# Moving routing steps inside the attention phase of a two-block kernel, with its inputs loaded four items ahead

## The chip, the cores and the metric

The kernel runs on one NeuronCore of a Trainium2 chip. The metric is the device time of one execution in microseconds (us). The engines are named as in the profile: PE is TensorE (the matrix engine; PEld is its weight loading), DVE is VectorE, ACT is ScalarE, POOL is GpSimd, SP is SyncE, which here only issues transfers. SBUF is the on-chip memory of 128 partitions, PSUM the accumulator memory that PE writes.

## The reference

Two blocks follow one another. The first is a linear attention with a decaying state (4 batches, 8 heads, 768 tokens, head size 48). The second is a mixture of 8 experts in which a token either takes the expert with the largest logit, or keeps the expert of the token before it.

```python
for t in range(S):                                  # attention, per batch and head
    cur = einsum('bhd,bhe->bhde', u * k[t], v[t])
    y[t] = einsum('bhd,bhde->bhe', r[t], state + cur)
    state = w * state + einsum('bhd,bhe->bhde', k[t], v[t])
x = y as (B, S, H*D)                                # 4 x 768 tokens of 384
...
logits = x @ w_gate                                 # 8 per token
local_gate = sigmoid(x @ w_local)
for b, s:                                           # the choice of an expert
    fresh_e = argmax(logits[b, s])
    e = fresh_e if s == 0 or local_gate[b, s] < 0.5 else prev_e
    prev_e = e
    p = softmax(logits[b, s])
    out[b, s] = p[e] * (relu(x[b, s] @ w1[e]) @ w2[e])
```

## The kernel before

The order of all work is written out by hand: each engine executes its instructions in the order in which the program emits them, and waits by semaphores for the others.

**Attention** (class Attention, method run) works through 16 items; an item is one batch and two heads. The loop runs over steps n = 0 to 16. Step n finishes item n-1 (`inside`, line L297; `before`, L310, whose result ACT copies at L318), turns the output of item n-2 (`turn`, L329, copied by ACT at L331), makes the score products of item n+1 (`scores`, L288, masked by DVE into the tile `am`, L290), starts item n's output (`own`, L267, multiplied by DVE into `y`, L273), scales keys two items ahead (`keys`, DVE, tile `kw`, L236), makes per-chunk sums (`added`, PE, L248, into a part T of the PSUM tile `mp`) and scans them to states (`states`, DVE, tile `S`, L254). POOL does `scale` for the next item: `rw` (L229), `ke` (L212) and `pd` (L216), two instructions each. The scores and the turned outputs share two PSUM banks (`pair`), so `turn` (L329) can only start once DVE has masked the scores that lay in its bank.

**Loads.** SP issues three transfers per item: `rk`, `kv`, `vT` (L194, L198, L199). `AHEAD` is the depth: there are AHEAD buffers of `rk` and of `vT` and AHEAD+1 of `kv`, and step n issues the loads of item n+AHEAD-1. In the kernel before AHEAD is 3. The queue is in order: a load whose buffer isn't free holds up those behind it.

**Routing** (class Router). Logits of a batch are made by PE every fourth step (`logits`, L342, then `token_logits`, L348 and the DVE reduction L349). Batches 0 and 1 form group 0, and its routing is spread over the steps 9 to 15 (g = 8 in the code): step 9 `experts_of` part 0 (L688 maximum, into `mp`; L689 comparison; L691 ACT copy of the maximum; L692 product with the table `down`), and part 1 (L694 to L696); step 10 `keys` (transposition L703) and `runs` (a scan, L708, from PSUM); step 11 `turn_runs` (L713, into `mp`), `last` (L720) and `one_hot` (L727 to L731); step 12 `counts` (two products, L740 and L741) and `ranks` (L747 to L756); step 13 `slots` (L792 to L795) and `columns` (tile `eqv`, L800); then `places` (tile `ohq`, L811, in two halves), `numbers` (tile `val`, L805, on POOL in step 14) and in step 15 `summed` (L818), `head` (L828 to L849) and the gather of the first expert's rows (L1077). Tables of whole numbers (`ie`, `iq`, `ij`, `down`, `t8`, `t1`, `tie`, `ief`) are made by POOL with iota instructions (L623) in steps 3, 4 and 5 (method `constants`), and cast to float by ACT in step 6 (L678).

**Experts** (class Experts) begin with the first gathered rows (transposed at L1090), products L1104, L1191, L1154, L1223, rows written by POOL (L1303). Group 1 (batches 2 and 3) is routed by the same methods while the first experts run. Weights of the first expert are loaded by SP in steps 14 and 15 (L1066).

Of the kernel before, what the change touches and what calls it, by code (L numbers as in the profile page):

```python
# [14 lines left out]
Alu = mybir.AluOpType  # L15
# [5 lines left out]
P = 128  # L21
# [5 lines left out]
E, F = 8, 1024  # L27
DK, FK = D // P, F // P
NCH = S // P
NC = B * NCH  # L30
N = B * S

ST = 4
# [4 lines left out]
EARLY = 2  # L38
HEAD = 192
TAIL = 256  # L40
# [8 lines left out]

W_LO, W_HI = 0.8, 1.25  # L50
C2 = NCH // 2
AHEAD = 3
VB = NCH * 2 * DH


def spread(ap, axis, n):

    a = ap.unsqueeze(axis)
    return a.to_broadcast([n if i == axis else s for i, s in enumerate(a.shape)])


class Attention:
# [289 lines left out]
    def run(self, router, fetch, heads):  # L352


        def pair(name):
            t = self.banks(name)
            return [t[:, 0], t[:, 1]]

        M = B * HP

        mp, mp_end = router.mp, 2 * P + 2 + (NCH - 1) * DH

        g = GROUPS[0][1] * HP
        for n in range(M + 1):
            if n + AHEAD - 1 < M:
                self.load(n + AHEAD - 1)
            if n == 0:
                self.scale(0)
                self.keys(0)
                self.tables()  # L370
                self.scores(0, 0)()
                self.scores(0, 1)()
                self.own(0)
                self.nc.scalar.copy(self.first, self.tab[:, 1, 0])
                self.turn_ends(slice(1, HP))
                self.warm(3)
                self.added(0)
                self.reciprocals(1)
                self.states(0)
                self.scale(1)  # L380
                continue
            if n < 3:

                self.keys(n)
                self.inside(n - 1)
                self.before(n - 1)
                if n == 2:
                    self.turn(0, pair("tp"))
                self.nc.scalar.copy(self.first, self.tab[:, n + 1, 0])
                self.scores(n, 0)()  # L390
                keep = self.scores(n, 1)
                self.own(n)
                keep()
                self.added(n)
                self.states(n)
                if n == 1:
                    self.reciprocals(2)
                self.scale(n + 1)
                continue
            if n < M:  # L400
                self.turn(n - 2, pair("tp"))
                if n >= M - 2:
                    fetch(2 * (n - M + 2))
                if n == 3:
                    self.reciprocals(3)
                if n < 5:
                    self.keys(n)
                if n > 3:
                    if n not in (g + 3, g + 5):
                        self.added(n)  # L410
                    self.states(n)
            if n == 4:
                self.keys(5)
            if n > HP and n % HP == 1:
                self.token_logits(n // HP - 1, pair("lq")[0])
            if n == g + 1:
                router.experts_of(0, (0,))
            if n == g + 5:
                router.slots(0)
                router.columns(0)  # L420
            if n == M:
                router.shares(0)
            if n + 1 < M:
                self.scale(n + 1)
            if n == g + 6:
                router.numbers(0, self.nc.gpsimd)
            if 3 <= n < 6:
                router.constants(n - 3)
            if n == M:
                self.turn(M - 2, [self.spare[:, 0], self.spare[:, 1]])  # L430
            self.inside(n - 1)
            if n == g + 3:

                router.turn_runs(0, mp[:, mp_end:])
            self.before(n - 1)
            if M - 2 <= n < M:
                fetch(2 * (n - M + 2) + 1)
            if n == 6:
                router.cast()
            if n == M:  # L440
                break
            if n == g + 3:
                router.last(0, mp[:, mp_end:])
                router.one_hot(0, (0,))
            if n == g + 7:

                router.summed(0, 0)
                router.copied(0, self.nc.vector.tensor_copy)
                self.spare = self.py.tile([P, 2, 512], F32, name="y")
                router.head(self.spare[:, 0])  # L450
                heads()

            ahead = n if n < 5 else n + 1
            if n == 3:
                self.added(3)
                self.states(3)
            if ahead < M:
                self.scores(ahead, 0)()
                keep = self.scores(ahead, 1)
            if n % HP == 0:  # L460

                keep()
                self.own(n)
                self.logits(n // HP - 1, pair("lp")[0])
                if n == 4:
                    self.scores(5, 0)()
                    self.scores(5, 1)()
                    self.keys(6)
                if n == g + 4:
                    self.added(n + 1)  # L470
                    router.counts(0, [mp, mp[:, E * NC // 2:]])
                    router.ranks(0, (0,))
                if n > 4:
                    self.keys(n + 2)
                if n == g + 4:
                    router.ranks(0, (1,))
            else:
                self.own(n)
                if n == g + 2:
                    self.added(n + 1)  # L480
                    router.keys(0, mp)
                    router.runs(0)
                if 4 < n < M - 2:
                    self.keys(n + 2)
                if ahead < M:
                    keep()
            if n == g + 1:
                router.experts_of(0, (1,))
            if n == g + 3:
                router.one_hot(0, (1,))  # L490
            if n == g + 5:
                router.places(0, 0)
            if n == g + 6:
                router.places(0, 1)
        self.inner.close()
# [81 lines left out]
class Router:  # L577
# [43 lines left out]
    def iota(self, name, shape, pattern, base=0, cm=0, cast=False):  # L621
# [5 lines left out]
        self.casts.append((f, i))  # L627
        return f

    def constants(self, part):  # L630
        nc = self.nc
        if part == 0:
            self.ie = self.iota("ie", [P, E], [[1, E]])
            self.iq = self.iota("iq", [P, P], [[1, P]])
            self.ij = self.iota("ij", [P, E * ST], [[1, E * ST]])
            self.ones = self.tl("r_ones", [P, P])
            nc.vector.memset(self.ones, 1.0)
        elif part == 1:
            self.down = self.iota("down", [P, E], [[-1, E]], base=E, cast=True)

            self.t8 = self.iota("t8", [P, NC], [[E * P, NC]], base=2 * E, cm=E, cast=True)
            self.t1 = self.iota("t1", [P, NC], [[P, NC]], base=1, cm=1, cast=True)
        else:

            c = self.g[0]["nc"]
# [5 lines left out]
            nc.vector.memset(self.go, 1.0)  # L651
            nc.vector.memset(self.go.rearrange("p (b c) -> p b c", c=NCH)[:, :, NCH - 1:], 0.0)
            nc.vector.memset(self.g[0]["ext"][:, :, 0:1], 0.0)

            self.tie = self.tl("tie", [P, E])
            for x, (z, base) in enumerate(((slice(0, EARLY), E - 1 - E * TAIL), (slice(EARLY, E), E - 1 - EARLY))):
                i = self.iota(f"tie{x}", [P, z.stop - z.start], [[-1, z.stop - z.start]], base=base)
                self.casts.append((self.tie[:, z], i))
            self.ief = self.iota("ief", [1, E], [[1, E]], cast=True)

            self.size = self.tl("size", [1, E])
            for i, n in enumerate(BLOCKS):
# [18 lines left out]
    def experts_of(self, i, parts=(0, 1)):  # L681

        nc, g, lt = self.nc, self.g[i], self.lt
        lg = lt[:, g["z"], :E]
        if 0 in parts:
            nc.vector.memset(lt[:, g["z"]].rearrange("p (b c) e -> p b c e", c=NCH)[0:1, :, 0, E:], -1.0)
            mx = self.mp[:, :g["nc"]] if i == 0 else g["mx"]
            nc.vector.tensor_reduce(mx, lg, axis=AX.X, op=Alu.max)  # L688
            nc.vector.tensor_tensor(g["eq"], lg, spread(mx, 2, E), op=Alu.is_equal)  # L689
            if i == 0:  # L690
                nc.scalar.copy(g["mx"], mx)  # L691
            nc.vector.tensor_tensor(g["eq"], g["eq"], spread(self.down, 1, g["nc"]), op=Alu.mult)  # L692
        if 1 in parts:
            nc.vector.tensor_reduce(g["k"], g["eq"], axis=AX.X, op=Alu.max)  # L694
            nc.vector.tensor_tensor(g["k"], self.t8[:, g["z"]], g["k"], op=Alu.subtract)
            nc.vector.scalar_tensor_tensor(g["key"], lt[:, g["z"], E], FRESH_TO, g["k"],  # L696
                                           Alu.is_le, Alu.mult)
# [1048 lines left out]
```

## Time and profile before

| what | value |
|---|---|
| median of 3 runs | 384.6 us (382.99 to 389.75) |
| the profiled execution's own time | 384.6 us |
| its span, first to last instruction | 382.8 us |
| mean granted TensorE clock | 0.995 |
| busy: PE | 366.8 us (96%) |
| busy: DVE | 251.9 us (66%) |
| busy: POOL | 151.9 us (40%) |
| busy: ACT | 107.3 us (28%) |
| moved by DMA | 74.97 MB, mean 196 GB/s |

The profiled execution has the time of the median; 1.8 us of it lie outside the span. The busy time of PE is modelled from pipelined products, so a busy PE is not always PE at its best. Attention takes the first 112 us or so; the experts' first products (L1104) start at 115.03 us.

### The profile page before, as it was taken

The page shows a single profiled execution, that of the slowest core. Times are in us where ns is not written, and L with a number is a line of the kernel's source. Part 1 is how long each engine was busy: PE and PEld are TensorE (multiplying, and loading weights), DVE is VectorE, ACT ScalarE, POOL GpSimd, SP SyncE. Part 2 cuts the span into 40 slices and gives each one's busy share as a digit, 9 for nine tenths or more (in the row PEclk, how much of TensorE's full clock was granted, in tenths as well). Part 3 has the DMA queues.
Part 4 walks back from the last instruction along what each step waited for, and adds up shares of the span by engine and source line. Part 5 has one row for each costly group of instructions (what it writes and reads, how often), then busy time and mean ns, then how long its engine had stood idle before and what let it go on. Part 6 is the DMA issues. An engine that isn't in the chain of part 4 may idle for free. (4 is left out here: it accounts for less than half of the span.)

```text
span 382.8 us, 9693 instructions
## 1 busy us (share of the span) xinstructions
PE 366.8 (96%) x3846; PEld 324.0 (85%) x3846; DVE 251.9 (66%) x720; ACT 107.3 (28%) x295; POOL 151.9 (40%) x213
## 2 busy tenths in 40 slices
PE   8999999889999999999999999999999999999992
PEld 7776777666769988999999999999999899899971
DVE  6888778988944646496566857758758758466400
ACT  4132232223222211322323333233234233232210
POOL 7769999887222042411432313213313113012022
PEclk9999999999999999999999999999999999999998
DMA  7999899977566880830561254145246146064011
GB/s 254 412 410 377 300 340 323 374 283 276 191 208 218 324 341 16 309 120 22 207 207 62 57 188 197 54 172 206 76 165 228 37 176 229 10 216 169 3 37 36
DMA packets 17765, 74.97 MB, mean 196 GB/s; under 512 B 2761, under 2 KB 6618, under 8 KB 15408
## 3 DMA queue, kind: packets, MB, share of 16 engines
q1 hardware_dynamic: 10336, 56.89, 40.4%
q0 software_dynamic: 3424, 9.52, 7.5%
q10 hardware_dynamic: 3952, 7.87, 5.7%
q8 instruction: 32, 0.52, 0.5%
q14 instruction: 21, 0.17, 0.2%
HBM read 64.83 MB, written 9.51 MB: 194 GB/s over the span
## 5 line engine op out<-in xcount | busy, mean ns | idle before, releaser
L1303 POOL DMA_INDIRECT out_dram<-yo,sid x27 | 26.7, 987 | 102.3 <-ACT yo L1298 78.9
L1154 PE MATMUL h<-exT,w1t 128*128 128x168 f32 (+4 forms) x240 | 54.9, 327 | 0.0
L1158 DVE TENSOR_TENSOR hT<-h,hs 128x168 f32<-128x168 f32 (+3 forms) x60 | 21.1, 351 | 46.5 <-PE h L1154 31.0
L1077 POOL DMA_INDIRECT xg<-x_d,gid x29 | 31.1, 1074 | 37.1 <-DVE sm L900 17.4
L1154 PEld LDWEIGHTS h<-exT,w1t 128*128 128x128 f32 x240 | 41.6, 190 | 0.3 <-issue 0.3
L1104 PE MATMUL h<-exT,w1t 128*128 128x192 f32 (+1 forms) x192 | 38.3, 338 | 0.0
L1223 PE MATMUL y<-factors,sums 128*128 128x192 f32 x168 | 36.8, 326 | 0.0
L1154 PE MATMUL h<-xs,ws 128*128 128x168 f32 (+4 forms) x144 | 35.2, 326 | 0.0
L216 POOL TENSOR_TENSOR pd<-rk 128x384 f32<-128x384 f32 x32 | 31.5, 1004 | 6.8 <-PE y L267 5.6
L290 DVE TENSOR_TENSOR am<-pair,kept 128x768 f32<-128x768 f32 x32 | 30.0, 951 | 5.9 <-PE pair L288 5.6
L1104 PEld LDWEIGHTS h<-exT,w1t 128*128 128x128 f32 x192 | 32.2, 190 | 1.5 <-issue 0.2
L1154 PEld LDWEIGHTS h<-xs,ws 128*128 128x128 f32 x144 | 25.5, 190 | 4.3 <-ACT hs L1161 1.2
L1223 PEld LDWEIGHTS y<-factors,sums 128*128 128x128 f32 x168 | 28.9, 190 | 0.0
L212 POOL TENSOR_TENSOR ke<-kv,endT 128x288 f32<-128x288 f32 x32 | 25.1, 803 | 1.5 <-DMA kv<-in_kv_dram 1.1
L229 POOL TENSOR_TENSOR rw<-rk,tab 128x384 f32<-128x384 f32 x26 | 23.8, 936 | 4.1 <-DMA rk<-in_rk_dram 4.1
L297 PE MATMUL y<-am,kv 128*64 128x128 f32 x360 | 23.9, 277 | 0.8 <-DVE y L273 0.8
L288 PE MATMUL pair<-rw,kw 48*64 48x128 f32 (+1 forms) x768 | 23.3, 250 | 1.1 <-DVE lt L349 0.6
L1223 PE MATMUL y<-w2t,hT 128*128 128x192 f32 x96 | 23.0, 328 | 0.0
L1091 DVE COPY exT<-tp 128x384 f32<-128x384 f32 (+6 forms) x29 | 14.0, 489 | 13.6 <-PE tp L1090 13.4
L288 PEld LDWEIGHTS pair<-rw,kw 48*64 48x64 f32 x768 | 19.5, 133 | 3.5 <-issue 1.9
L297 PEld LDWEIGHTS y<-am,kv 128*64 128x64 f32 x360 | 19.9, 137 | 2.4 <-DVE y L273 1.0
L318 ACT COPY xT<-y 128x768 f32<-128x768 f32 x15 | 12.0, 800 | 33.7 <-PE y L310 33.7
(300 smaller groups left out, 741.7 us busy)
## 6 DMA issues: line engine op xcount, KB each, us to landing
w1t<-in_w_dram SPq DMA_DIRECT2D x8, 1536.0 KB, 6.7
w2t<-in_w_dram SPq DMA_DIRECT2D x8, 1536.0 KB, 7.5
rk<-in_rk_dram SPq DMA_DIRECT2D x15, 768.0 KB, 7.4
kv<-in_kv_dram SPq DMA_DIRECT2D x16, 584.0 KB, 7.1
vT<-in_vT_dram SPq DMA_DIRECT2D x16, 384.0 KB, 6.7
x_d<-x ACTq DMA_DIRECT2D x4, 1152.0 KB, 4.6
w1t<-in_w_dram SPq DMA_DIRECT2D x2, 768.0 KB, 4.6
w2t<-in_w_dram SPq DMA_DIRECT2D x2, 768.0 KB, 4.5
```

The lines of the kernel that those rows point to most:

```text
L212: nc.gpsimd.tensor_mul(t["ke"][:, p::2], t["k"][:, p::2], spread(self.endT[:, p, hp], 1, C2))
L216: nc.gpsimd.tensor_mul(t["pd"][:, z], t["rT"][:, z], t["kT"][:, z])
L229: engine.tensor_mul(t["rw"][:, z], t["rT"][:, z], spread(pw, 1, z.stop - z.start))
L288: nc.tensor.matmul(sc[f * DP:(f + 1) * DP, h, i, x:], lhsT=t["kw"][q, c, o * DP:(o + 1) * DP], rhs=t["rw"][q, c, x:], start=True, stop=True)
L290: return lambda: nc.vector.tensor_mul(t["am"][:, g], sc, spread(self.kept[:, g:g + 3], 1, 2))
L297: nc.tensor.matmul(t["y"][h][p * DP:(p + 1) * DP, c2 * P:(c2 + 1) * P], lhsT=t["v"][:, (2 * c + h) * DH:(2 * c + h) * DH + DP], rhs=t["am" ...
L1077: self.nc.gpsimd.indirect_dma_start(out=xg[:n], out_offset=None, in_=self.x_d[:rows], in_offset=bass.IndirectOffsetOnAxis(ap=u["gid"][:n, ...
L1104: nc.tensor.matmul(h[:, :n], lhsT=u["w1"][:, m, kk, :], rhs=u["xT"][:, kk, :], start=(kk == 0), stop=(kk == DK - 1))
L1154: nc.tensor.matmul(out, lhsT=a, rhs=b, start=start and k == 0, stop=stop and k == len(terms) - 1, skip_group_check=True)
L1158: nc.vector.tensor_tensor(out, a, b, op=Alu.add)
L1223: return lambda: nc.tensor.matmul(bank[:, x * half:(x + 1) * half], lhsT=a, rhs=b, start=(j == 0 and x == 0), stop=(j == FK // 2 - 1), ski ...
L1303: self.nc.gpsimd.indirect_dma_start(out=out.rearrange("n (h d) -> (n h) d", h=2) if half else out, out_offset=bass.IndirectOffsetOnAxis(ap ...
```

## The change

Six things are altered:

- AHEAD becomes 4: one more buffer of `rk`, `vT` and `kv`, and each load is issued one step earlier in the program; the load of `wp` (weights of the logits) comes after the loads of item 2.
- In `experts_of` for group 0 the result of the comparison (L689) goes to PSUM, into a free part of `mp`, and the product (L692) reads it there.
- The scan of states of item 11 (step 11) is emitted in step 10, right behind the scan `runs`.
- In step 12 `added` and `counts` are emitted ahead of `logits`.
- In step 13 `columns` (`eqv`) moves from the start of the step to its end, behind the second masking, and the first half of `places` moves from there into step 14, behind the scan of states.
- All iota tables are made in step 2, between `states` and `scale`, in a method `numbering`; `constants` keeps its DVE memsets in steps 3 and 5.

```diff
-AHEAD = 3
+AHEAD = 4
...
                 if n == 1:
                     self.reciprocals(2)
+                else:
+                    router.numbering()
                 self.scale(n + 1)
...
                     if n not in (g + 3, g + 5):
                         self.added(n)
-                    self.states(n)
+                    if n != g + 3:
+                        self.states(n)
...
             if n == g + 5:
                 router.slots(0)
-                router.columns(0)
...
             if n == g + 6:
                 router.numbers(0, self.nc.gpsimd)
-            if 3 <= n < 6:
+                router.places(0, 0)
+            if n in (3, 5):
                 router.constants(n - 3)
...
                 self.own(n)
+                if n == g + 4:
+                    self.added(n + 1)
+                    router.counts(0, [mp, mp[:, E * NC // 2:]])
                 self.logits(n // HP - 1, pair("lp")[0])
...
                 if n == g + 4:
-                    self.added(n + 1)
-                    router.counts(0, [mp, mp[:, E * NC // 2:]])
                     router.ranks(0, (0,))
...
                     router.keys(0, mp)
                     router.runs(0)
+                    self.states(n + 1)
...
             if n == g + 5:
-                router.places(0, 0)
+                router.columns(0)
...
+    def numbering(self):
+        self.ie = self.iota("ie", [P, E], [[1, E]])
+        self.iq = self.iota("iq", [P, P], [[1, P]])
+        self.ij = self.iota("ij", [P, E * ST], [[1, E * ST]])
+        self.down = self.iota("down", [P, E], [[-1, E]], base=E, cast=True)
+        self.t8 = self.iota("t8", [P, NC], [[E * P, NC]], base=2 * E, cm=E, cast=True)
+        self.t1 = self.iota("t1", [P, NC], [[P, NC]], base=1, cm=1, cast=True)
+        self.tie = self.tl("tie", [P, E])
...
+        self.ief = self.iota("ief", [1, E], [[1, E]], cast=True)
...
-            nc.vector.tensor_tensor(g["eq"], lg, spread(mx, 2, E), op=Alu.is_equal)
+            eq = self.mp[:, g["nc"]:g["nc"] * (E + 1)].rearrange("p (c e) -> p c e", e=E) if i == 0 else g["eq"]
+            nc.vector.tensor_tensor(eq, lg, spread(mx, 2, E), op=Alu.is_equal)
             if i == 0:
                 nc.scalar.copy(g["mx"], mx)
-            nc.vector.tensor_tensor(g["eq"], g["eq"], spread(self.down, 1, g["nc"]), op=Alu.mult)
+            nc.vector.tensor_tensor(g["eq"], eq, spread(self.down, 1, g["nc"]), op=Alu.mult)
```

More of the change, by code (lines that the diff above doesn't have):

```diff
@@ L628, in iota @@
         return f
+    def numbering(self):
[6 more added lines that the diff above has]
+        self.tie = self.tl("tie", [P, E])
+        for x, (z, base) in enumerate(((slice(0, EARLY), E - 1 - E * TAIL), (slice(EARLY, E), E - 1 - EARLY))):
+            i = self.iota(f"tie{x}", [P, z.stop - z.start], [[-1, z.stop - z.start]], base=base)
+            self.casts.append((self.tie[:, z], i))
+        self.ief = self.iota("ief", [1, E], [[1, E]], cast=True)
     def constants(self, part):
@@ L632, in constants @@
         if part == 0:
-            self.ie = self.iota("ie", [P, E], [[1, E]])
-            self.iq = self.iota("iq", [P, P], [[1, P]])
-            self.ij = self.iota("ij", [P, E * ST], [[1, E * ST]])
             self.ones = self.tl("r_ones", [P, P])
             nc.vector.memset(self.ones, 1.0)
[L638 to L642, printed above, removed]
         else:
@@ L653, in constants @@
             nc.vector.memset(self.g[0]["ext"][:, :, 0:1], 0.0)
[L655 to L659, printed above, removed]
             self.size = self.tl("size", [1, E])
```

## The prediction

> **What bounds the kernel now.** I first cut the span into stages by the busy time of each engine. Columns: stretch, its length, then busy time and instruction count of PE, PEld, DVE, ACT, POOL, then granted clock, DMA share, GB/s.
>
> ```profile
> 0.00:115.00 115.00, 106.91 (x2203) 81.76 (x2203) 91.63 (x167) 32.19 (x81) 87.93 (x124) 1.00 0.86 312
> 115.00:376.00 261.00, 259.91 (x1645) 242.22 (x1643) 160.29 (x554) 75.10 (x214) 63.02 (x88) 1.00 0.42 149
> 376.00:382.80 6.80, 0.00 (x0) 0.00 (x0) 0.00 (x0) 0.00 (x0) 0.97 (x1) 0.73 0.09 21
> ```
>
> The experts (115 to 376 us) leave PE idle for 1.1 us of 261: PE sets their length, and an earlier start of them is an earlier end. The change touches nothing there. In attention PE is idle for 8.1 us of 115, and only there can a new order win. So I cut attention into steps, from the first `before` product (L310) of a step to that of the next one: steps 9 to 14.
>
> ```profile
> 66.40:72.71 6.31, 5.31 (x128) 4.19 (x126) 6.31 (x6) 1.50 (x3) 5.37 (x7) 1.00 1.00 356
> 72.71:79.27 6.56, 5.66 (x131) 4.47 (x129) 6.17 (x11) 1.50 (x3) 4.98 (x7) 1.00 0.99 371
> 79.27:85.80 6.53, 5.67 (x129) 4.51 (x129) 5.13 (x8) 1.88 (x5) 6.28 (x8) 1.00 0.66 250
> 85.80:93.40 7.60, 7.60 (x151) 5.46 (x150) 5.85 (x8) 2.22 (x5) 6.89 (x9) 1.00 0.70 257
> 93.40:100.17 6.77, 5.41 (x129) 4.32 (x127) 6.53 (x16) 1.57 (x4) 3.21 (x4) 1.00 0.53 183
> 100.17:105.45 5.28, 5.28 (x129) 4.24 (x127) 4.77 (x6) 1.65 (x5) 0.00 (x0) 1.00 0.84 282
> ```
>
> Step 14 (last row) has PE busy throughout and takes 5.28 us, as do the plain steps 6 and 7 (L310 at 48.56, 53.84, 59.12): that is PE's own floor. Step 12 carries the logits and counts and also has no idle PE. Steps 9 and 13 have DVE nearly full and PE waiting: there DVE is the bound. In the timeline I then looked for what PE waits for, and what DVE does ahead of it.
>
> ```profile
> 65.85 1.68 POOL L229 TENSOR_TENSOR rw<-rk,tab 128x384 f32<-128x384 f32 x2
> 66.13 3.03 DVE L692 TENSOR_TENSOR eq<-eq,down 128x96 f32<-128x96 f32 x1
> 67.50 1.54 POOL L212 TENSOR_TENSOR ke<-kv,endT 128x288 f32<-128x288 f32 x2
> 70.08 0.79 PE L329 MATMUL pair<-ident,xT 112*128 112x112 f32 x6 [1.00 <-DVE am L290]
> ...
> 79.11 0.23 PE L713 MATMUL mp<-ident,run 12*128 12x12 f32 x1 [0.90 <-DVE inc L726]
> 83.17 0.79 PE L329 MATMUL pair<-ident,xT 112*128 112x112 f32 x6 [0.86 <-DVE am L290]
> 91.41 1.08 DVE L748 TENSOR_TENSOR_SCAN exc<-seg,ext 128x104 f32<-128x104 f32 x1 [1.52 <-ACT ext L747]
> 95.38 0.77 PE L288 MATMUL pair<-rw,kw 48*64 48x128 f32 x24 [0.63 <-DVE lt L349]
> 96.05 0.56 DVE L800 TENSOR_TENSOR eqv<-si,ij_i 128x384 f32<-128x384 int32 x1
> 97.53 0.80 PE L329 MATMUL pair<-ident,xT 112*128 112x112 f32 x6 [0.73 <-DVE am L290]
> ...
> 115.67 0.26 DVE L689 TENSOR_TENSOR eq<-lt,mx 128x96 f32<-128x96 f32 x1
> 115.96 0.26 DVE L692 TENSOR_TENSOR eq<-eq,down 128x96 f32<-128x96 f32 x1
> ```
>
> The reader is to see that L692 takes 3.03 us at 66.13 and 0.26 us at 115.96, where POOL does nothing. The long one ends (69.16) just after POOL's unbroken row of `rw` and `ke` (69.04). Its two inputs both lie in SBUF. DVE instructions with one input in PSUM stay at their time beside a busy POOL: the scans L254 between 60 and 112 us take 0.630 to 0.655 us. PE's waits for DVE in these steps add up to 1.00 + 0.90 + 0.86 + 0.63 + 0.73 = 4.12 us. That is the stock that this change can draw on.
>
> **The change part by part.**
>
> *Comparison in PSUM (step 9).* Instruction counts stay; L692 now has one SBUF input. At 0.26 instead of 3.03 us, DVE is 2.77 us earlier. As built, L692 now also waits for ACT's copy L691 (0.17 us), so some 0.2 comes off. PE had waited 1.00, and the step exceeds the floor by 6.31 - 5.28 = 1.03: gain 1.00. Bounds: 0, if L692 is slow for another reason, and 1.03. The rest of the 2.77 makes DVE punctual in step 10, behind it.
> [...]
>
> *Scan behind the runs (steps 10, 11).* The transposition L713 writes `mp` and waited 0.90 us until DVE had done the scan L254 (78.42 to 79.05), though PE was free at 78.2 and `runs` was done at 76.78. With the scan right behind `runs` it ends at 76.78 + 0.64 = 77.42, before PE is free: gain 0.90. Queued behind it on DVE are `kw` and one masking, 0.64 us later each, done by about 79.1; the next to need them is L288 at 80.42, less the 0.90. Hidden, with 0.4 us of cover. The wait of 0.86 in step 11 stands behind L728 and L729, which take 0.68 and 0.72 us there against 0.17 alone; they collide with `ke` on POOL, and that is changed by nothing here except its timing. Between 0 and 0.86, I take 0.3, nearer the row as it is.
>
> *Counts in front of logits (step 12).* The order on PE changes, not its work. The logits hold it for 1.50 us (L342 from 88.41), so the counts come that much earlier and the 1.52 us in which DVE waits for `ext` go. But behind it come L754 to L756 (0.25, 0.18 and 0.26 us), with SBUF inputs, and `ke` holds POOL from 92.22 to 93.85: they may end where they end now. Logits come 0.8 us later; ACT's copy (0.48 us) then ends about when L348 is due, 91.5, so this costs up to 0.1.
>
> *`eqv` behind the masks (steps 13, 14).* It frees 0.56 us ahead of the masking for which PE waits 0.73, and puts them into step 14, where DVE has 5.28 - 4.77 = 0.51 us free. There `ohq` (0.95 us) may also stand behind `val` on POOL, which now can't begin before `eqv` and takes 0.83. Together with the counts: at best all of 0.63 + 0.73 = 1.36 goes and step 14 gives back 0.05, so 1.3; at worst only 0.56 goes and 0.05 + 0.83 comes back, so -0.3. Of these I take 0.6, near the middle. What becomes late next is the masking at the start of step 14, and L329 behind it.
>
> *Tables in step 2.* Nine iotas take 0.40 + 0.29 + 0.26 = 0.95 us of POOL by their rows at 33.44, 38.94 and 44.62. They move into this wait:
>
> ```profile
> 22.25 1.69 POOL L229 TENSOR_TENSOR rw<-rk,tab 128x384 f32<-128x384 f32 x2 [2.25 <-DMA rk<-in_rk_dram]
> ```
>
> They cost nothing there. If the load came earlier and took that cover away, POOL's `pd` of item 3 would end 0.95 later than 27.38, still before its use at 29.07. In steps 3 to 5 POOL gains 0.95, but no matrix product waits for POOL: taken as 0, at most 0.6 (weight loads waited that long for `ke`).
>
> *Four items ahead.* No bytes are added: an item is 768 + 584 + 384 = 1736 KB. POOL waits for loads 4.1 (`rw`), 1.2 (`pd`) and 1.1 us (`ke`) in all, and those go. But POOL is ahead: the `rw` that waits 1.15 us at 79.02 is used by PE at 86.33. Gain 0. On SP, the loads of items 0 and 1 keep their places, `wp` goes behind item 2 and isn't used before 36.22. Against it: from 12 to 30 us DMA moves 411 to 413 GB/s without a gap, and another item in flight (4.3 us at that rate) can hold up item 3. Were all 4.3 added to `rw` at 22.25, `pd` would end at 31.7 instead of 27.4, 2.6 us after its use. Bounds 0 and a loss of 2.6; I take 0, since the loads are issued in order.
>
> *Sum:* 1.0 + 0.9 + 0.3 + 0.6 = 2.8 us of the profiled execution, which at 384.6 us is the median itself: 381.8 us.
>
> **The rivals.**
>
> *All of it goes.* Every wait of the 4.12 vanishes, since the parts help each other: 384.6 - 4.1 = 380.5. For it: DVE has less work than PE in all six steps together once the collisions are gone. Against it: `eqv` finds a full step, and L728 and L729 still collide.
>
> *L692 doesn't get faster.* For it: L696, L731 and L748 got in at the next end of a POOL instruction, while L692 let three go by, so perhaps its place and not POOL held it. Then 1.0 is missing: 382.8.
>
> *POOL without gaps, on the slower side.* With AHEAD at 4 POOL never waits for a load, and runs `rw`, `ke` and `pd` without the gaps of 0.73, 0.43 and 1.15 us by which DVE slips in at 72 to 80 us. The routing instructions with two SBUF inputs (L695, L696, L728, L731, L748, L755, L756) are then held as L692 was. One such hold cost PE 1.00 in step 9 and helped to the 0.90 in step 10, so 1.9. It decides from two holds on (3.8 against 2.8); three make 384.6 - 2.8 + 5.7 = 387.5. Against it: `pd` still waits for `own` (5.6 us in 5 waits now), which leaves gaps.
>
> **How the numbers follow.** The forecast has a chance of 0.6 (own range 380.5 to 383.5, the bounds of steps 11 to 14), all of it 0.17, L692 as slow as now 0.11, POOL without gaps 0.12. The likeliest gives 381.8. The range of 378.8 to 386.0 goes to 1.7 below the first rival, for the steps 1 to 4, which are over the floor too, and to the bound of 2.6 us of loss on the other side with part of the last rival. A difference of 2%, 7.7 us, is about what a measurement of this kernel can tell from no change. Faster than that would need nearly all of PE's idle time in attention: 0.05. Slower needs (7.7 + 2.8) : 1.9, five or six such holds, or early loads starved for several items: 0.07. Within 2%: 0.88.
>
> **What would show it.** Right: L692 at about 0.26 us in step 9 and L329 there without its wait; L713 without the 0.90; L748 about 1.5 us sooner after L267; iotas between 20 and 22 us; a first L1104 at about 112.2 instead of 115.03, and the same 261 us behind it. Wrong: L692 still near 3; L728, L731 or L748 above 1.5 us; a wait of L329 in step 14 of more than 1 us; PE waiting for POOL or DMA between 14 and 36 us; or a longer stage of experts.

## The result and the profile after

| | before | after |
|---|---|---|
| median of 22 runs each | 383.77 us (382.94 to 389.75) | 382.29 us (381.38 to 383.43) |
| the profiled execution's own time | 384.6 us | 382.2 us |
| its span | 382.8 us | 380.4 us |
| first expert product (L1104 before, L1109 after) | 115.04 us | 112.59 us |

The ratio of the times is 0.9943, with a 95% interval of 0.9923 to 0.9964: 0.6% faster, within the 2% that the forecast called no change. The medians are only 1.48 us (0.4%) apart: the ratio answers to the averages (384.62 and 382.44 us, without the one execution of 389.75), since 9 of the other 21 executions of the kernel before, but none of the changed kernel, took over 384 us. The forecast was 381.8 us. The two traces differ by 2.45 us at the first expert product and by 2.4 us at the end, so the stage of experts is as long as it was.

From the comparison (L689) on, line numbers are five higher in the kernel after (L692 became L697, L713 L718, L748 L753, `ohq` L811 L816). First the steps 9 to 14 by windows from L310 to L310, with the columns of the forecast's first view, and the experts from a start 3 us earlier:

```profile
66.33:71.61 5.28, 5.28 (x129) 4.23 (x127) 3.69 (x5) 1.50 (x3) 3.47 (x5) 1.00 0.92 325
71.61:77.20 5.59, 5.59 (x131) 4.47 (x129) 5.52 (x11) 1.50 (x3) 5.59 (x7) 1.00 1.03 412
77.20:83.46 6.26, 6.00 (x130) 4.69 (x129) 5.50 (x9) 1.89 (x5) 4.98 (x7) 1.00 0.91 351
83.46:91.29 7.83, 7.83 (x151) 5.52 (x149) 5.51 (x9) 2.12 (x5) 7.83 (x10) 1.00 0.11 40
91.29:97.18 5.89, 5.41 (x129) 4.32 (x127) 5.67 (x15) 1.57 (x4) 2.21 (x3) 1.00 0.58 202
97.18:103.08 5.90, 5.31 (x129) 4.19 (x127) 5.90 (x9) 1.65 (x5) 0.83 (x1) 1.00 0.83 269
112.00:373.70 261.70, 260.45 (x1648) 242.66 (x1648) 161.14 (x556) 75.00 (x214) 62.83 (x88) 1.00 0.42 149
```

Step 9 is at the floor of 5.28 that the forecast read from step 14; step 14 itself has left the floor, with DVE busy for all of its 5.90 us. The lines of the timeline that answer to those shown of before:

```profile
20.86 1.68 POOL L229 TENSOR_TENSOR rw<-rk,tab 128x384 f32<-128x384 f32 x2 [0.22 <-DMA rk<-in_rk_dram]
...
66.32 0.26 DVE L697 TENSOR_TENSOR eq<-mp,down 128x96 f32<-128x96 f32 x1 [0.29 <-ACT mx L696]
68.93 0.79 PE L329 MATMUL pair<-ident,xT 112*128 112x112 f32 x6
77.04 0.23 PE L718 MATMUL mp<-ident,run 12*128 12x12 f32 x1
78.11 1.56 POOL L212 TENSOR_TENSOR ke<-kv,endT 128x288 f32<-128x288 f32 x2
78.74 0.95 DVE L733 TENSOR_TENSOR ei<-inc,rn 128x12 int32<-128x12 f32 x1
88.82 0.48 ACT L343 COPY lT<-pair 128x384 f32<-128x384 f32 x1 [3.62 <-PE pair L342]
89.20 0.24 ACT L752 COPY ext<-mp 128x96 f32<-128x96 f32 x1
89.48 0.70 DVE L753 TENSOR_TENSOR_SCAN exc<-seg,ext 128x104 f32<-128x104 f32 x1 [1.93 <-ACT ext L752]
93.06 0.77 PE L288 MATMUL pair<-rw,kw 48*64 48x128 f32 x24 [0.42 <-DVE lt L349]
97.18 0.55 DVE L805 TENSOR_TENSOR eqv<-si,ij_i 128x384 f32<-128x384 int32 x1
97.87 0.83 POOL L810 TENSOR_TENSOR val<-eqv,t 128x384 f32<-128x384 f32 x1 [1.27 <-DVE eqv L805]
98.21 1.31 DVE L816 TENSOR_TENSOR ohq<-si,iq_i 128x768 f32<-128x768 int32 x1
100.44 0.80 PE L329 MATMUL pair<-ident,xT 112*128 112x112 f32 x6 [0.59 <-DVE am L290]
```

L697 takes 0.26 us; L329 in step 9 and L718 have no wait left. But DVE waits longer for `ext` than before (1.93 against 1.52 us), and L329 has a new wait of 0.59 in step 14, behind an `ohq` of 1.31 us.

### The profile page after: what moved, and what is told of

Read it like the earlier page. It is cut to its first block, busy times and chain, and to the rows that moved or that the text cites. A ratio compares the mean times of both kernels' runs of the same rounds, so it can differ in the third digit from the quotient of the medians.

```text
span 380.4 us, 9693 instructions
## 1 busy us (share of the span) xinstructions
PE 366.9 (96%) x3846; PEld 323.9 (85%) x3846; DVE 248.7 (65%) x720; ACT 107.1 (28%) x295; POOL 151.3 (40%) x213
## 5 line engine op out<-in xcount | busy, mean ns | idle before, releaser
L1109 PE MATMUL h<-exT,w1t 128*128 128x192 f32 (+1 forms) x192 | 38.3, 338 | 0.0
L1109 PEld LDWEIGHTS h<-exT,w1t 128*128 128x128 f32 x192 | 32.3, 190 | 1.5 <-issue 0.2
```

What stands on the lines that cost most here:

```text
L1109: nc.tensor.matmul(h[:, :n], lhsT=u["w1"][:, m, kk, :], rhs=u["xT"][:, kk, :], start=(kk == 0), stop=(kk == DK - 1))
```

## The experiments

Every kernel ran beside the kernel before, in three groups, in which the kernel before had a median of 383.39 us (b_psum, a_sbuf, a_scan, a_counts), 385.33 us (b_ahead4, a_eqv, a_ext, a_early) and 383.86 us (the others); so a time is read by its ratio. The kernels' differences are about as large as the intervals of the ratios, so the parts are judged by the length of the steps, in one trace of each kernel. Kernels that are alike in these steps differ by up to 0.2 us in step 10 (5.59 to 5.77) and 0.3 in step 11 (6.16 to 6.45), and less than that says nothing. Steps 9 to 15, from L310 to L310, in us:

| kernel | 9 | 10 | 11 | 12 | 13 | 14 | 15 | sum |
|---|---|---|---|---|---|---|---|---|
| before | 6.31 | 6.56 | 6.53 | 7.60 | 6.77 | 5.28 | 5.51 | 44.56 |
| after | 5.28 | 5.59 | 6.26 | 7.83 | 5.89 | 5.90 | 5.43 | 42.18 |
| b_psum | 5.28 | 7.27 | 6.33 | 7.60 | 6.76 | 5.28 | 5.51 | 44.03 |
| b_ahead4 | 5.88 | 6.73 | 5.66 | 7.60 | 6.66 | 5.28 | 5.52 | 43.33 |
| a_sbuf | 5.29 | 5.59 | 6.26 | 7.84 | 5.83 | 5.90 | 5.44 | 42.15 |
| a_ahead3 | 5.28 | 5.70 | 6.50 | 13.43 | 5.43 | 5.89 | 5.44 | 47.67 |
| a_scan | 5.28 | 6.58 | 5.65 | 7.85 | 5.94 | 5.90 | 5.43 | 42.63 |
| a_rn | 5.28 | 5.78 | 6.00 | 7.84 | 5.97 | 5.89 | 5.44 | 42.20 |
| a_counts | 5.28 | 5.77 | 6.16 | 7.60 | 6.08 | 5.90 | 5.44 | 42.23 |
| a_eqv | 5.28 | 5.59 | 6.26 | 7.84 | 6.54 | 5.28 | 5.51 | 42.30 |
| a_ext | 5.28 | 5.59 | 6.26 | 7.85 | 5.44 | 5.89 | 5.44 | 41.75 |
| a_early | 5.28 | 5.59 | 6.25 | 9.07 | 6.79 | 5.28 | 5.52 | 43.78 |
| a_ohq | 5.29 | 5.59 | 6.45 | 7.84 | 5.95 | 5.28 | 6.38 | 42.78 |
| a_best | 5.28 | 5.58 | 6.20 | 7.84 | 5.52 | 5.28 | 6.39 | 42.09 |

### Step 9: the comparison and the depth of the loads

**b_psum**: the kernel before with the result of the comparison in PSUM, and nothing else changed.

```diff
-nc.vector.tensor_tensor(g["eq"], lg, spread(mx, 2, E), op=Alu.is_equal)
+eq = self.mp[:, g["nc"]:g["nc"] * (E + 1)].rearrange("p (c e) -> p c e", e=E) if i == 0 else g["eq"]
+nc.vector.tensor_tensor(eq, lg, spread(mx, 2, E), op=Alu.is_equal)
...
-nc.vector.tensor_tensor(g["eq"], g["eq"], spread(self.down, 1, g["nc"]), op=Alu.mult)
+nc.vector.tensor_tensor(g["eq"], eq, spread(self.down, 1, g["nc"]), op=Alu.mult)
```

> The kernel before, with the comparison's result in PSUM and nothing else changed. If POOL held the product with two SBUF inputs (theory), the product takes 0.26 us instead of 3.03, step 9 falls from 6.31 to 5.28 us, and step 10 gains part of its 0.9 as well, since DVE arrives there 1.4 us earlier: in all 1.0 to 1.9 us. If its place and not POOL made it slow (rival), it stays near 3.0 us and no step changes.

Measured: 383.78 us, ratio 0.9986 (0.9951 to 1.002).

```profile
65.40 0.26 DVE L693 TENSOR_TENSOR eq<-mp,down 128x96 f32<-128x96 f32 x1 [0.29 <-ACT mx L692]
...
73.22 0.87 PE L267 MATMUL y<-pd,w_t 48*64 48x384 f32 x7 [0.20 <-issue]
```

The product falls to 0.26 us and step 9 to 5.28, by 1.03: one input in PSUM is enough, and the rival that its place makes it slow falls. An input in PSUM didn't lengthen the comparison either: in the kernel before L689 took 0.254 us with its maximum there (at 65.84) and 0.258 with it in SBUF (at 115.67). The whole time doesn't show it: the interval holds both no change and the 1.0 us expected. Step 10 gained nothing: the transposition still waits 0.89 us for DVE (0.90 before), so that DVE was earlier in step 9 didn't make the scan punctual. Step 10 even lost 0.7 us to something that this edit doesn't touch: PE stood still in the middle of L267 (first product at 72.48, the next at 73.22), marked "issue". I come back to that.

**b_ahead4** (the kernel before, AHEAD 4 alone) and **a_sbuf** (the changed kernel, the comparison back in SBUF).

> The kernel before with AHEAD 4 alone. Theory: POOL no longer waits for loads, runs 1.7 us earlier in step 9, and the product with both inputs in SBUF is held only until POOL rests, 1.5 us instead of 3.0; DVE is then in time for the masking and step 9 falls from 6.31 to 5.3 us by the loads alone, with the waits of steps 10 to 13 as before: 1.0 us faster. Rival (the prediction): four ahead is worth nothing, step 9 stays at 6.3.

> The changed kernel, with the comparison's result back in SBUF and nothing else changed. POOL works there until 67.37 us (rw, then ke, whose first half ends at 66.6), then waits till 69.18; the product is due at 66.06. Held until POOL rests: it ends near 67.5 and takes about 1.4 us; the masking behind it is due only at 67.72, so steps 9 and 10 keep 5.28 and 5.59 us and the time stays that of the changed kernel. Let in at the next end of a POOL instruction: 0.8 us, and no change either. Slow by its place or by itself: 3.0 us, step 9 back near 6.3 us, 1 to 2 us lost.

Measured: b_ahead4 383.26 us, ratio 0.9963 (0.9925 to 1.0); a_sbuf 381.52 us, 0.9943 (0.9905 to 0.9981). The same instruction in each, with POOL beside it:

```profile
65.19 1.68 POOL L229 TENSOR_TENSOR rw<-rk,tab 128x384 f32<-128x384 f32 x2
65.90 2.59 DVE L692 TENSOR_TENSOR eq<-eq,down 128x96 f32<-128x96 f32 x1
66.83 1.54 POOL L212 TENSOR_TENSOR ke<-kv,endT 128x288 f32<-128x288 f32 x2
```

```profile
65.72 1.55 POOL L212 TENSOR_TENSOR ke<-kv,endT 128x288 f32<-128x288 f32 x2
65.87 1.52 DVE L696 TENSOR_TENSOR eq<-eq,down 128x96 f32<-128x96 f32 x1
```

In b_ahead4 the product ends 0.12 us after `ke` (68.49 against 68.37), in a_sbuf also 0.12 after it (67.39 against 67.27): held until POOL rests. In a_sbuf the masking that follows is due only at 67.61, when PE has made its scores, so the hold costs nothing and the steps 9 and 10 are as in the changed kernel: with the rest of the change in place POOL is further on, rests sooner, and the edit in PSUM no longer brings anything. POOL begins this `rw` 0.55 us ahead of the step's first L310 in the kernel before, 0.98 in b_ahead4 and 2.06 in a_sbuf. In a_ahead3 (below), with the early tables and without the depth, it is 0.97, so each brings 0.4 us of lead and both together 1.5 (the other kernels with both: 1.65 to 2.42 us ahead); no run moved the tables alone. The depth alone brings step 9 to 5.88, between its theory (5.3) and its rival (6.3). PSUM and POOL's full lead each cure step 9; they don't add.

b_ahead4 wins more two steps later, where no expectation looked for it:

```profile
78.47 1.56 POOL L212 TENSOR_TENSOR ke<-kv,endT 128x288 f32<-128x288 f32 x2
80.33 0.17 DVE L728 TENSOR_TENSOR ei<-inc,rn 128x12 int32<-128x12 f32 x1
```

The maximum L728 comes 0.30 us behind `ke` and takes 0.17 us, where the kernel before had it inside `ke` with 0.68 (and L729 with 0.72), and step 11 falls by 0.87. In its trace the depth alone shortens the steps 9 to 15 by 1.23 us, half of what the whole change does.

**a_ahead3**: the changed kernel with AHEAD back at 3.

> The changed kernel with AHEAD back at 3. Theory (the comparison in PSUM and the depth of the loads cover each other in the steps 9 and 10): step 9 stays at 5.28 with the product L697 at 0.26, step 10 within 0.4 of 5.59, POOL waits for loads again (rw 4 us in all), the first L1104 is within 0.4 us of the changed kernel's and the ratio to the kernel before about 0.995. Rival (the depth by itself is what the change lives on): the steps 9 to 11 lose 1 us or more, the ratio is 0.998 or above. A second rival (loads issued earlier cost something in the steps 1 to 5): these steps get shorter by more than 0.5 us in all.

Measured: 382.99 us, ratio 0.9985 (0.9945 to 1.0026). The steps 9 and 10 are at 5.28 and 5.70, as the theory has it, and the steps 1 to 5 (34.6 us) say nothing on depth: the kernels with four items ahead span 34.7 to 35.6, those with three 34.5 to 35.5. But step 12 is 5.6 us longer:

```profile
82.86 2.00 POOL L229 TENSOR_TENSOR rw<-rk,tab 128x384 f32<-128x384 f32 x2
82.88 5.50 DVE L736 TENSOR_TENSOR oh<-ei,ie_i 128x96 f32<-128x96 int32 x1
84.81 1.56 POOL L212 TENSOR_TENSOR ke<-kv,endT 128x288 f32<-128x288 f32 x2
86.32 1.95 POOL L216 TENSOR_TENSOR pd<-rk 128x384 f32<-128x384 f32 x2
88.30 0.64 DVE L254 TENSOR_TENSOR_SCAN S<-step,mp 128x240 f32<-128x240 f32 x1
...
89.05 0.40 PE L248 MATMUL mp<-kv,ke 128*48 128x48 f32 x4 [3.31 <-POOL pd L216]
```

L736 takes 0.51 us in the changed kernel. Here it began together with `rw` and was held through six POOL instructions, to 0.11 us behind the last of them (88.27). The wait of PE is put down to `pd`; what ended last for it was the scan L254 on DVE, which reads `mp`, stands behind L736 and ran from 88.30 to 88.94. This is one execution (its own time 386.1 us), and no expectation had it. Whether an instruction like this slips in at the first end on POOL (as in the changed kernel) or waits for the whole row is worth 5 us here, more than any part of the change. The ratio lies where the rival put it (0.998 or above; the interval holds the theory's 0.995 too), but not for its reason: the steps 9 to 11 lose 0.35 us, not 1.

The executions over 384 us go with the depth, too. With the longest left out as above, 52 of 126 with three items ahead took that long (the kernel before 46 of 107, b_psum 3 of 10, a_ahead3 3 of 9), and 5 of 124 with four (b_ahead4 1 of 10, the changed kernel none of 22). So a part of the ratio is that they become rare, and this part belongs to AHEAD. Two of them have a trace, and each has a long hold: the kernel before (384.6 us, L692 for 3.03) and a_ahead3 (386.1, L736 for 5.50). That the others have such holds is possible, and open.

### Steps 10 and 11: the scan

**a_scan**: the changed kernel with the scan of item 11 back in step 11.

```diff
-                    if n != g + 3:
-                        self.states(n)
+                    self.states(n)
...
-                    self.states(n + 1)
```

> The changed kernel, with the scan of states of item 11 back in step 11. Theory: the transposition of the runs writes mp and waits for the scan, which stands behind kw and a masking and ends near 78.15 us instead of 76.26, so the transposition starts at 78.2 instead of 77.04 and 1.0 us is lost. Rival: with DVE punctual since step 9 the scan is done in time anyway, and less than 0.3 us is lost.

Measured: 381.98 us, ratio 0.9953 (0.9922 to 0.9984). Step 10 is 0.99 longer, and the wait ahead of the transposition (L716 here) is back with 0.93. But step 11 is 0.61 shorter:

```profile
78.30 0.23 PE L716 MATMUL mp<-ident,run 12*128 12x12 f32 x1 [0.93 <-DVE inc L729]
78.38 1.56 POOL L212 TENSOR_TENSOR ke<-kv,endT 128x288 f32<-128x288 f32 x2
80.00 0.17 DVE L731 TENSOR_TENSOR ei<-inc,rn 128x12 int32<-128x12 f32 x1
```

The maximum comes 0.06 us after `ke` and takes 0.17; in the changed kernel it comes inside `ke` and takes 0.95. The theory was right on step 10; over the steps 10 and 11 the scan part is worth 0.38 net: two thirds of what it wins in step 10 are lost to POOL in step 11.

**a_rn**: the changed kernel, the maximum of step 11 with one input in PSUM.

```diff
-router.turn_runs(0, mp[:, mp_end:])
+router.turn_runs(0, mp)
...
+g["rt"] = bank[:, :g["nc"]] if i == 0 else g["rn"]
...
-nc.vector.tensor_tensor(g["ei"][:, 0], g["inc"][:, :g["nc"]], g["rn"], op=Alu.max)
+nc.vector.tensor_tensor(g["ei"][:, 0], g["inc"][:, :g["nc"]], g["rt"], op=Alu.max)
```

> The changed kernel, with one input of the maximum in one_hot (tile ei, step 11) read from PSUM, where the transposition of the runs left it, instead of from ACT's copy in SBUF; the transposition goes to another part of mp for that. Theory (a DVE instruction with two SBUF inputs is held by POOL's instruction, one with an input in PSUM isn't): the maximum takes 0.17 to 0.25 us beside ke instead of 0.95, the masking behind it begins 0.7 us earlier, and step 11 falls from 6.26 to about 5.65, the length that it has where the maximum doesn't meet ke; first L1104 0.6 earlier, at 112.0. Rival (the length of 0.95 comes from something else in the place, or the next wait stands right behind it): the maximum stays above 0.6, or step 11 stays above 6.1.

Measured: 381.37 us, ratio 0.9928 (0.9895 to 0.9961).

```profile
78.09 1.56 POOL L212 TENSOR_TENSOR ke<-kv,endT 128x288 f32<-128x288 f32 x2
78.76 0.17 DVE L734 TENSOR_TENSOR ei<-inc,mp 128x12 int32<-128x12 f32 x1
78.96 0.72 DVE L735 TENSOR_SCALAR ei<-ei 128x12 int32<-128x12 int32 x1
79.60 0.94 DVE L290 TENSOR_TENSOR am<-pair,kept 128x768 f32<-128x768 f32 x1
```

The maximum falls to 0.17 as the theory has it, and the instruction behind it, which takes 0.17 in the changed kernel, is held in its place: 0.72. It has one input, so "two inputs in SBUF" was too narrow. Nor was each instruction that reads SBUF alone held beside POOL: in the changed kernel the reduction L699 took 0.24 us inside an `rw` and 0.25 at 113.8 us. Step 11 gains 0.26 instead of 0.6, no more than alike kernels differ by (a_best, with the same edit, has 6.20), and step 10 is 0.19 longer in the same trace: nothing is left of it in the sum.

### Steps 12 to 15: counts, `eqv`, `ohq`

**a_counts**: the changed kernel, `added` and `counts` behind the logits again. **a_eqv**: the changed kernel, `columns` at the start of step 13 and the first half of `places` at its end again.

> The changed kernel, with the counts behind the logits again. Theory (from the trace of the changed kernel): ACT copies the counts (ext) only after its copy of the logits, which it was given first, so counts in front brought DVE nothing; putting them back leaves the start of the scan exc about 3.8 us behind the first own product of step 12 (4.2 now), step 12 goes from 7.83 to about 7.6 us and step 13 stays within 0.2 of 5.89: 0.0 to 0.4 us faster. Rival (the prediction's step): exc starts up to 1.5 us later and step 13 loses 0.6 us or more.

> The changed kernel, with eqv back at the start of step 13 and the first half of ohq back at its end. Theory: this part only moves DVE's 0.56 us from step 13 into step 14, which had 0.51 free, and lets ohq collide with val on POOL (1.31 instead of 0.95 us): put back, step 13 grows from 5.89 to about 6.4 us and step 14 falls from 5.90 to 5.28, together within 0.2 of now. Rival (the prediction): the part gained 0.3 us or more, so the two steps together grow by that.

Measured: a_counts 381.4 us, ratio 0.9945 (0.9912 to 0.9977); a_eqv 382.5 us, 0.993 (0.989 to 0.997). Neither part is worth anything by itself, as both theories had it. The steps 12 to 14 take 19.62 us in the changed kernel and 19.58 with the counts back. The steps 13 and 14 take 11.79, and 11.82 with `eqv` back: step 13 loses 0.65, step 14 wins 0.62.

**a_ext**: the changed kernel, ACT's copy of the counts and the scan behind it in front of the logits too.

```diff
                     router.counts(0, [mp, mp[:, E * NC // 2:]])
+                    router.ranks(0, (0,))
                 self.logits(n // HP - 1, pair("lp")[0])
...
-                if n == g + 4:
-                    router.ranks(0, (0,))
```

> The changed kernel, with the copy ext and the instructions exc and pos also emitted in front of the logits. Theory: ACT then copies the counts before the logits, exc starts right behind y, about 1.7 us sooner, the wait of 0.42 us for the logits' reduction in step 13 goes, and DVE's lag in step 14 shrinks: 0.5 to 1.0 us faster than the changed kernel, first expert product near 111.9 us. Rival: the copy of the logits comes 0.24 us later on ACT, the turn of the logits waits for it, and collisions with POOL take back the rest: 0.2 us or less.

Measured: 381.99 us, ratio 0.9925 (0.9897 to 0.9954).

```profile
87.52 0.24 ACT L751 COPY ext<-mp 128x96 f32<-128x96 f32 x1 [2.17 <-PE mp L745]
87.79 0.89 DVE L752 TENSOR_TENSOR_SCAN exc<-seg,ext 128x104 f32<-128x104 f32 x1
...
89.82 0.37 DVE L758 TENSOR_SCALAR far<-pos 128x24 f32<-128x24 f32 x1
90.23 0.72 DVE L759 TENSOR_TENSOR pos<-pos,far 128x24 f32<-128x24 f32 x1
90.99 0.80 DVE L760 TENSOR_TENSOR pos<-pos,oh 128x96 f32<-128x96 f32 x1
```

The wait for `ext` is gone, and `exc` begins 2.38 us after the first L267 of its step (85.41) instead of 4.23. So the cause is ACT's queue: in the changed kernel the copy `ext` stands behind the copy of the logits, which waits for the logits that now come later. The three small instructions that follow run into `ke` and take 1.89 us instead of 0.69, which takes back 1.2; step 13 still falls to 5.44. By the sum of its steps this is the shortest of all kernels, 0.43 below the changed one, between the two expectations; the interval of its time doesn't separate the two.

**a_early**: a_ext with `slots` and `columns` already in step 12, the first half of `places` at the end of step 13.

> As the kernel with ext in front of the logits, and slots and eqv already in step 12, the first half of ohq at the end of step 13. DVE has about 2 us free in step 12 and none in steps 13 and 14. Theory: step 12 stays within 0.2 of 7.83, step 13 falls from 5.89 to 5.3 to 5.5, step 14 from 5.90 to 5.28: 1.0 to 1.2 us faster than the changed kernel, first expert product near 111.5 us. Rival: with POOL busy throughout step 12, slots and eqv are held there and the masking of step 13 comes late: no better than the kernel with ext alone.

Measured: 382.88 us, ratio 0.9967 (0.993 to 1.0003). Against a_ext, step 12 grows by 1.2 us and step 13 by 1.35. In step 12, 1.08 us are a stall of PE itself:

```profile
86.12 0.21 PE L288 MATMUL pair<-rw,kw 48*64 48x64 f32 x1 [1.08 <-issue]
```

In step 13 the reduction L349 and the masking stand behind the new work and come later, with PE waiting 1.45 us for L349. Step 12 says nothing on the edit; step 13 is a loss, as the rival had it, while step 14 is at 5.28 as the theory had it.

**a_ohq**: the changed kernel, the first half of `places` behind the last masking of step 14. **a_best**: a_ext, a_ohq and a_rn together.

> The changed kernel, with the first half of the table ohq taken from the start of step 14 and emitted at its end, ahead of the second half; nothing else is altered. Theory (step 14 is long because 1.31 us of ohq, held by POOL's val, stand ahead of the masking for which L329 waits 0.59 us): the wait of 0.59 goes, ohq takes 0.95 alone, step 14 falls from 5.90 to 5.3, step 15 stays within 0.1 of 5.43, since the scan of states that now comes later is used only in step 16; the first L1104 at about 112.0 instead of 112.59. Rival (DVE has no idle time from 91 to 103 us, so the work only moves): step 14 falls, but step 15 gets the 0.6 back, since the products of summed wait for the table; first L1104 as now.

> The changed kernel with three edits: ACT's copy of the counts and the scan behind it (ranks, first part) in front of the logits, the first half of ohq at the end of step 14, and one input of the maximum in step 11 read from PSUM. Theory (the three waits are separate: 0.45 in step 13, 0.59 in step 14, 0.6 in step 11): the steps 11 to 14 sum to about 24.2 us instead of 25.88, the first L1104 is at about 111.0 if the steps 1 to 5 are as now, and the time is 1.6 us below the changed kernel's, 380.5 to 381, a ratio to the kernel before of about 0.990. Rival (what one part gains, the next step gives back): the sum of the steps 11 to 14 stays above 25.2.

Measured: a_ohq 381.9 us, ratio 0.9943 (0.9915 to 0.9971); a_best 381.34 us, 0.9939 (0.9909 to 0.9968).

```profile
101.87 1.81 DVE L816 TENSOR_TENSOR ohq<-si,iq_i 128x768 f32<-128x768 int32 x2
103.61 0.65 DVE L254 TENSOR_TENSOR_SCAN S<-step,mp 128x240 f32<-128x240 f32 x1
104.40 0.86 PE L823 MATMUL mp<-ohq,val 128*32 128x128 f32 x24 [0.88 <-DVE S L254]
```

In a_ohq step 14 falls to the floor as the theory has it, and step 15 takes 0.95 back: the product L823 writes `mp`, from which the scan L254 reads, and the scan now stands behind both halves of `ohq`. The rival was right on the time, though not on the reason: it named the table. In a_best the steps 11 to 14 take 24.84 us, between the two expectations, and step 15 then gives back the same 0.96; its first expert product also waits 0.60 for the gathered rows. From 91 to 103 us DVE has no room, and what is moved there comes out elsewhere.

## Why the prediction was right, and where not

The sign was right, and so was the size between the two traces: 2.45 us at the first expert product against 2.8 forecast. That 381.8 came out near the median of 382.29 is in part luck: the forecast's base, 384.6, lay 0.8 us above the median of 22, and between the medians the change brought 1.48 us, about half of 2.8. By its terms (differences of the step lengths in the two traces):

| term | forecast | measured |
|---|---|---|
| step 9, comparison in PSUM | 1.0 | 1.03 |
| step 10, scan behind the runs | 0.9 | 0.97 |
| step 11, small collisions | 0.3 | 0.27 |
| steps 12 to 14, counts and `eqv` | 0.6 | -0.23 + 0.88 - 0.62 = 0.03 |
| steps 1 to 8, step 15, the start | 0 | 0.15 |

**The step that failed** is "the counts come that much earlier and the 1.52 us in which DVE waits for `ext` go". The counts did come earlier on PE; `ext` didn't, because ACT makes it, in order, behind the copy of the logits. I followed the move through PE's queue and not through ACT's, and the wait grew to 1.93. a_ext shows it. The result lies inside the term's bounds (-0.3 to 1.3); my value of 0.6 missed it, as almost nothing came. The price feared for `eqv` was right in kind: `ohq` behind `val` took 1.31 instead of 0.95, and a new wait of 0.59 came up in step 14.

**Right in the whole, not in the sharing.** The 1.03 of step 9 was put down to the comparison in PSUM, and AHEAD was taken as 0. b_psum shows that the first is enough, a_sbuf that the rest of the change is enough without it, and b_ahead4 that the depth alone is worth 1.23 us over the steps 9 to 15. So the sum came out by parts that replace each other. I looked at what four items ahead would hold up, and not at where it would put POOL's row in time. That an earlier L692 makes DVE punctual in step 10 failed too: in b_psum the wait there stays at 0.89. The scan's 0.97 is real, but a_scan gives it a net worth of 0.38, since it also moves the maximum of step 11 into `ke`: in a_scan, without that, step 11 wins 0.88 instead of 0.27. That 0.3 was forecast for this step and 0.27 came is luck: POOL's place decides it, and with the maximum just behind `ke` it is 0.9 (a_scan, b_ahead4).

**The nothings.** The tables lie at 19.69 to 20.64 us and are hidden as forecast (step 2: 6.83 against 6.82); behind them `rw` still waits 0.22 for its load. POOL's waits for loads didn't all go: `rw` waits 0.2 us instead of 4.1, but `pd` 2.4 instead of 1.2 and `ke` 1.8 instead of 1.1. L753 doesn't begin 1.5 us sooner, as the list of signs wanted. Most of what makes up the 0.15 of the other steps isn't the change's: step 3 wins 0.54 by a stall of PE that the traced execution of before had at 28.23 and none of the other kernels had there, b_psum, which does the same work up to there, among them. Steps 4 and 5 lose 0.10 and 0.31 (step 5 takes 5.59 to 5.87 with four items ahead, 5.28 to 5.45 with three; the cause isn't shown).

**The rivals.** All of it goes: it didn't, since DVE is full in the steps 13 to 15. POOL without gaps: POOL waits less for loads (4.4 us in all against 6.4), but the holds in the changed kernel stay below 1 us. The longest hold, 5.50 us, appeared with three items ahead. The rival had the mechanism, but set it in the wrong kernel, and its price of 1.9 us for a hold was far below the 5 us of this one.

## What to carry to other kernels

Follow a moved instruction through every queue that its result passes, the copying engine's too: what comes earlier on PE isn't earlier for its user if the copy stands behind something late (here the wait for `ext` grew from 1.52 to 1.93 us). A small DVE instruction between SBUF operands was priced here by where POOL's row was when it arrived (the maximum of step 11 took 0.68 us inside `ke` in the kernel before, 0.17 behind it in b_ahead4), so an edit that only shifts POOL can do the same as one that moves the operand (0.17 inside `ke` in a_rn), and the two don't add (step 9: 5.28 us in b_psum, 5.29 in a_sbuf, 5.28 with both). Where one engine was full over two or three steps, moving its work only moved the wait (a_eqv: step 13 0.65 us longer, step 14 0.62 shorter); test each part by undoing it alone and by making it alone, on the step lengths: a part that looks worth nothing when it is undone can be covered by another.

## What the runs showed of the hardware

**Holds over a whole row.** DVE instructions with SBUF operands, held by POOL, took 1.52 (a_sbuf), 2.59 (b_ahead4), 3.03 (the kernel before) and 5.50 us (a_ahead3), through up to six POOL instructions with pauses of less than 0.1 us, and each ended 0.11 or 0.12 us behind the last of them. Without such a hold the product took 0.26 us (b_psum, and L692 at 115.96 in the kernel before) and L736 0.51 (the changed kernel). So an instruction of DVE was held past several ends of POOL's. Which end lets it in isn't settled. The long hold came with a lower clock: the granted TensorE clock of a_ahead3's step 12 was 0.75 (1.00 in the changed kernel), and its 16 logits products took 2.79 us instead of 1.50.

**Stalls of PE behind an instruction packet.** In 13 places of the fourteen traces PE or its weight load stood 0.3 to 1.3 us with "issue" as the releaser, at places that only some of the kernels have in common. Each of these stalls ended 1.2 to 1.6 us after a packet of 16,384 bytes had ended in the instruction queue that the profile lists:

```profile
q8 instruction: 32, 0.52, 0.6%
```

(packets, MB, share of 16 engines, in the changed kernel; such a packet comes every 4 to 9 us in attention). The stalls of before at 28.23, of b_psum at 73.22 and of a_early at 86.12 are among them; that of before is 0.47 us of the weight load, 1.43 behind a packet, and in the changed kernel the weight load stood for 0.37 us up to 79.80, 1.45 behind one. If PE waits there for what the packet brings, one such stall costs as much as a part of this change (0.27 us in step 11). This is not shown: it rests on the times of the records, no experiment moved a packet, and waits marked "issue" also recur at fixed places, at other distances from a packet: the weight load of L329 near 63 us (0.62 us in 13 of the 14 traces) starts 3.67 us behind one in the kernel before and 3.20 in the changed kernel. Those are not counted here.
